# Dealing the tokens nine to a partition pair, loading the first batch in head halves, and a reordered first chain

## The chip, the cores and the metric

The kernel runs on one core of a Trainium2 chip. The metric is the device time of one execution in microseconds (us). The engines named here are PE (TensorE matmuls; PEld is its weight load), DVE (VectorE), ACT (ScalarE), POOL (GpSimd) and SP (SyncE, which only issues DMAs). Sixteen DMA engines serve all queues of the core. SBUF has 128 partitions; a "lower" tile lies in partitions 0 to 63, an "upper" one in 64 to 127.

## The reference

Eight batches, eight heads, 576 tokens, head size 64; then a mixer with rank 32 along the tokens and a hidden width of 2048.

```python
r = max(x, 0);  phi(x) = [r * cos(pi/2 * s/S), r * sin(pi/2 * s/S)]   # s: the token's position
kv  = einsum('bhsf,bhsd->bhfd', phi(k), v);  z = sum_s phi(k)
x   = einsum('bhsf,bhfd->bhsd', phi(q), kv) / (phi(q) . z + 1e-6)     # then [B, S, H*D]
u   = x + (x^T @ U @ V)^T                                            # U [576, 32], V [32, 576]
out = u + max(u @ w_ch1, 0) @ w_ch2                                  # [512 x 2048], [2048 x 512]
```

All inputs and the output are float32 in DRAM; matmuls run in bf16.

## The kernel before, in words

**Tokens.** 576 tokens are four and a half times 128. A batch is held as four chunks of 128 tokens and a tail of 64. Token 4p+c (p below 128, c below 4) is partition p of chunk c; tokens 512 to 575 are the tail, chunk 4, which lies in the lower partitions for even batches and the upper ones for odd batches, so that two batches share one tail tile (`tail`, L49). Every q, k or v of a batch is loaded by SP in two DMAs: `load_main` (L74, issued at L75; 128 partitions x 8 heads, 1 KB runs) and `load_tail` (L80, issued at L81; 64 partitions x 8 heads, 256 B runs). They land in float32 staging tiles `qst/kst/vst` and `qt/kt/vt` with one buffer each, so a batch's load waits until the one before has been read.

**The attention of a batch.** `q_prep` and `k_prep` (L246, L240) write relu(x) times cos and sin as bf16. `v_prep` and `v_block` cast v into `v_ext`, which has a column of ones for the denominator. `qtr_unit` (L273) transposes q on PE. `kv_unit` (L252) makes kv of four heads, `den_unit` and `recip` (L314, L310) the reciprocal denominators, `xh_unit` (L330) x for four heads of a chunk. `A_unit` (L374) multiplies by U, and `uTd_open`, `uTd_mm`, `uTd_evac` (L432 to L455) make the transposed u, which is what the mixer's first product reads.

**The mixer.** `g1_main` (L477, matmuls at L487) makes 16 tiles of the hidden layer of a batch from w_ch1 (`w1_bf`, four DMAs on POOL's queue at L91, cast to bf16 on the way), ACT applies the relu (L496). `g1_tail` (L500, matmuls at L507) does the shared tail of a pair. `g2_part` (L521, matmuls at L540) multiplies a chunk by w_ch2 (`w2_bf`, four DMAs at L97); DVE adds u (L550) into `o_sb` (four buffers), and one DMA per chunk writes 128 rows of 2 KB to `out` (L560), two DMAs of 64 rows for the shared tail (L556). The first three pairs write from POOL's queue; the last pair writes from SP's, and its last chunk in two parts, 384 columns from SP and 128 from ACT.

**The start.** The order is written by hand (`manual_schedule`), each engine works its own list from top to bottom. SP issues q, k, v of batch 0 (v in two halves of the heads), then V and U, then batch 1. POOL waits for k's tail (the copy into `mark`, L703), issues two of the four w_ch1 loads, casts V and U (`cast_uv`), issues the other two, then waits for k of batch 1 (L719) before the four w_ch2 loads. `chain_head`, `chain_mid` and `chain_end` (L645 to L685) are the first batch's attention, heads 0 to 3 ahead of heads 4 to 7, with `keep_warm` matmuls on zeros (L174) in the gaps of PE. Then `g1_main` of batch 0 starts. Later batches are laid beside the slots of the mixer by `attention_plan` and its table PLAN.

Of the kernel before, what the change touches and what calls it, by code (L numbers as in the profile page):

```python
# [17 lines left out]
def kernel(  # L18
# [29 lines left out]

    def tail(b):  # L49
        lo = TS * (b % 2)  # L50
        return slice(lo, lo + TS)
# [8 lines left out]
    kst, vst, qst, kt, vt, qt = {}, {}, {}, {}, {}, {}  # L60

    def alloc_k(b):
        kst[b] = pool.tile([P, H, 4, D], FP32, tag="kst", bufs=1, name="kst")
        kt[b] = pool.tile([P, H, D], FP32, tag="kt", bufs=1, name="kt")

    def alloc_v(b):
        vst[b] = pool.tile([P, H, 4, D], FP32, tag="vst", bufs=1, name="vst")
        vt[b] = pool.tile([P, H, D], FP32, tag="vt", bufs=1, name="vt")

    def alloc_q(b):  # L70
        qst[b] = pool.tile([P, H, 4, D], FP32, tag="qst", bufs=1, name="qst")
        qt[b] = pool.tile([P, H, D], FP32, tag="qt", bufs=1, name="qt")

    def load_main(dst, src, b, h0=0, h1=H, eng=None):  # L74
        (eng or nc.sync).dma_start(  # L75
            out=dst[:, h0:h1, :, :].rearrange("p h c d -> p h (c d)"),
            in_=src[b, h0:h1, 0:512, :].rearrange("h (p c) d -> p h (c d)", c=4),
        )

    def load_tail(dst, src, b, eng=None):  # L80
        (eng or nc.sync).dma_start(  # L81
            out=dst[tail(b), :, :],
            in_=src[b, :, 512:S, :].rearrange("h s d -> s h d"),
        )
# [16 lines left out]
    def cast(eng, o, i):  # L101
# [10 lines left out]

    alloc_k(0)
    alloc_q(0)
    alloc_v(0)
    iota = const.tile([P, 5], FP32)
    nc.gpsimd.iota(
        out=iota[:, 0:4], pattern=[[1, 4]], base=0, channel_multiplier=4,
        allow_small_or_imprecise_dtypes=True,
    )  # L120
    for lo in (0, TS):
        nc.gpsimd.iota(
            out=iota[lo : lo + TS, 4:5], pattern=[[1, 1]], base=512, channel_multiplier=1,
            allow_small_or_imprecise_dtypes=True,
        )
    load_main(qst[0], q, 0)
    load_tail(qt[0], q, 0)
    load_main(kst[0], k, 0)
    load_tail(kt[0], k, 0)
    load_tail(vt[0], v, 0)  # L130
    load_main(vst[0], v, 0, 0, 4)
    load_main(vst[0], v, 0, 4, 8)
    nc.sync.dma_start(out=stV, in_=moe_V)
    nc.sync.dma_start(
        out=stU[:, 0:4, :], in_=moe_U[0:512, :].rearrange("(p c) r -> p c r", c=4)
    )
    for lo in (0, TS):
        nc.sync.dma_start(out=stU[lo : lo + TS, 4, :], in_=moe_U[512:S, :])
# [7 lines left out]
    nc.scalar.activation(out=sinw, in_=iota, func=AF.Sin, bias=0.0, scale=scale_ang)  # L146
    nc.scalar.activation(out=cosw, in_=iota, func=AF.Sin, bias=halfpi, scale=-scale_ang)
# [14 lines left out]
    for i in range(2):  # L162
        V_.memset(v_ext[i][:, 4, :, :], 0.0)
        V_.memset(v_ext[i][:, 0:4, :, D:E], 1.0)
        V_.memset(v_ext[i][tail(i), 4, :, D:E], 1.0)
# [10 lines left out]
    V_.memset(U_bf, 0.0)  # L176
    mark = const.tile([TS, 1], FP32)
# [7 lines left out]
    def cast_uv():  # L185
        cast(G_, V_nat, stV)
        cast(G_, U_bf[:, 0:4, :], stU[:, 0:4, :])
        for i in range(2):
            cast(G_, U_bf[tail(i), 4 + i, :], stU[tail(i), 4, :])

    def spread_v(eng):
        v_ps = ps.tile([P, 2, 512], FP32, tag="X", bufs=1, name="v_ps")
        nc.tensor.matmul(
            out=v_ps[:, 0, :], lhsT=four, rhs=V_nat[:, 0:512], start=True, stop=True
        )
        nc.tensor.matmul(
            out=v_ps[:, 1, 0:TS], lhsT=four, rhs=V_nat[:, 512:S], start=True, stop=True
        )
        cast(eng, V_bf, v_ps[:, 0, :].rearrange("r (p c) -> r c p", c=4))
        cast(eng, V_tl, v_ps[:, 1, 0:TS])  # L200
# [5 lines left out]
    def v_prep(b, h0=0, h1=H, cs=range(5), engs=None):  # L206
        vx = v_ext[b % 2]
        for n, c in enumerate(cs):
            eng = engs[n] if engs else G_
            if eng is None:  # L210
                continue
            if c < 4:
                cast(eng, vx[:, c, h0:h1, 0:D], vst[b][:, h0:h1, c, :])
            else:
                cast(eng, vx[tail(b), 4, h0:h1, 0:D], vt[b][tail(b), h0:h1, :])

    def v_block(b, h0, h1, c0, c1, eng):
        cast(
            eng,
            v_ext[b % 2][:, c0:c1, h0:h1, 0:D].rearrange("p c h d -> p h c d"),  # L220
            vst[b][:, h0:h1, c0:c1, :],
        )
# [9 lines left out]
    def prep(dst, src, b, c, engs, h0, h1):  # L232
        rows = slice(0, P) if c < 4 else tail(b)
# [6 lines left out]
    def k_prep(b, c, engs, h0=0, h1=H):  # L240
        if b not in k_p:
            k_p[b] = pool.tile([P, 4, H, 2 * D], BF16, tag="k_p", bufs=1, name="k_p")
        src = kst[b][:, h0:h1, c, :] if c < 4 else kt[b][:, h0:h1, :]
        prep(k_p[b][:, c] if c < 4 else k_tl, src, b, c, engs, h0, h1)

    def q_prep(b, c, engs, h0=0, h1=H):  # L246
        if b not in q_p:
            q_p[b] = pool.tile([P, 4, H, 2 * D], BF16, tag="q_p", bufs=1, name="q_p")
        src = qst[b][:, h0:h1, c, :] if c < 4 else qt[b][:, h0:h1, :]
# [23 lines left out]
    def qtr_unit(b, c, h0=0, h1=H, eng=None, tag="T", bufs=1):  # L273
# [8 lines left out]
        if c < 4:  # L282
            cast(eng or V_, q_pT[b][:, c, h0:h1, :], t_ps[:, h0:h1, :])
        else:
            cast(eng or V_, q_tlT[:, h0:h1, tail(b)], t_ps[:, h0:h1, tail(b)])

    def qtr_dma(b, c0, c1):
# [6 lines left out]
        else:  # L294
            nc.sync.dma_start_transpose(
                out=q_tlT[:, :, tail(b)],
                in_=q_tl[tail(b), :, :].rearrange("p h f -> p (h f)"),
# [223 lines left out]
    def g2_part(pr, cc, part):  # L521
# [32 lines left out]
        if cc == 4:  # L554
            for i in range(2):
                eng.dma_start(  # L556
                    out=out[2 * pr + i, 512:S, :], in_=o_sb[i * TS : i * TS + TS, :]
                )
        else:
            eng.dma_start(  # L560
                out=out[b, 0:512, cols].rearrange("(p c) n -> p c n", c=4)[:, c, :],
# [4 lines left out]
    def loads(b, eng):  # L566
        def kk():
            alloc_k(b)
            load_tail(kt[b], k, b, eng)
            load_main(kst[b], k, b, eng=eng)  # L570

        def vv():
            alloc_v(b)
            load_tail(vt[b], v, b, eng)
            load_main(vst[b], v, b, eng=eng)

        def qq():
            alloc_q(b)
            load_tail(qt[b], q, b, eng)
            load_main(qst[b], q, b, eng=eng)  # L580

        return qq, kk, vv
# [21 lines left out]
    def attention_plan(b):  # L604
# [32 lines left out]
        for at, t in zip(lo, loads(b + 1, nc.sync) if lo else ()):  # L637
            plan.append((w + at, t))
# [6 lines left out]
    def chain_head(b, fill, xt, engs):  # L645
        v_prep(b, 0, 4, (4,), (engs[0],))
        v_block(b, 0, 4, 0, 3, V_)
        v_block(b, 0, 4, 3, 4, engs[0])
        kv_unit(b, 0, "T", 1)
        fill(0)  # L650
        rec0 = den_unit(b, 0, 4, "X", 1)
        v_prep(b, 4, 8, (4,), (A_,))
        v_block(b, 4, 8, 0, 4, A_)
        fill(1)
        for n, c in enumerate(ORD):
            xh_unit(b, c, 0, 4, rec0, *xt[n])
            if n == 1:
                fill(2)
            if n == 3:
                kv_unit(b, 1, "T", 1, A_)  # L660

    def chain_mid(b, fill, xt, dt):
        fill(3)
        m = 3
        rec1 = den_unit(b, 4, 8, *dt)
        for n, c in enumerate(ORD[:m]):
            xh_unit(b, c, 4, 8, rec1, *xt[n])
        u01 = ps.tile([P, 2, 512], FP32, tag="X", bufs=1, name="u01")
        uTd_open(b, 0, None, None, u01[:, 0, :].rearrange("p (c t) -> p c t", c=4))
        uTd_open(b, 1, None, None, u01[:, 1, :].rearrange("p (c t) -> p c t", c=4))  # L670
        a0 = A_unit(b, "T", 1, A_, 0, 256)
        fill(4)
        uTd_mm(b, 0)
        uTd_mm(b, 1)
        uTd_evac(b, 0, A_)
        uTd_evac(b, 1, A_)
        for n, c in enumerate(ORD[m:]):
            xh_unit(b, c, 4, 8, rec1, *xt[m + n])
        fill(5)
        return a0  # L680

    def chain_end(b, a0):
        A_unit(b, "T", 1, V_, 256, 512, a0)
        uTd_open(b, 2, "o", 2)
        uTd_open(b, 3, "o", 2)  # L685

    def warm0(n):
        m = (2, 1, 0, 1, 1, 2)[n]
        if m:
            keep_warm(m, *(O2 if n == 0 else G3))  # L690

    keep_warm(18, "X", 1)
    for c in TL:
        q_prep(0, c, (V_, V_ if c == 3 else A_))
    for n, c in enumerate(TL):
        qtr_unit(0, c, 0, H, (V_, A_, V_, A_, V_)[n], *(G3 if n < 3 else O2))
        if n in (1, 3):
            keep_warm(1, "X", 1)
    for c in TL:
        k_prep(0, c, (V_, V_ if c == 3 else A_))  # L700
    keep_warm(13, "o", 2)

    G_.tensor_copy(out=mark, in_=kt[0][0:TS, 0, 0:1])  # L703
    w1_load(0)
    w1_load(1)
    cast_uv()
    w1_load(2)
    w1_load(3)
    chain_head(0, warm0, (O2, O2, G3, G3, O2), (A_,))
    alloc_q(1)  # L710
    load_main(qst[1], q, 1)
    load_tail(qt[1], q, 1)
    alloc_k(1)
    load_tail(kt[1], k, 1)
    load_main(kst[1], k, 1)
    alloc_v(1)
    load_tail(vt[1], v, 1)
    load_main(vst[1], v, 1)
    G_.tensor_copy(out=mark, in_=kst[1][0:TS, 7, 3, 0:1])  # L719
    for n in range(4):  # L720
        w2_load(n)
    spread_v(A_)
    a0 = chain_mid(0, warm0, (O2, G3, O2, G3, O2), G3)
    chain_end(0, a0)
# [71 lines left out]
    for n, t in enumerate(loads(2, nc.sync)):  # L796
# [38 lines left out]
```

## Time and profile before

| | us |
|---|---|
| median of 3 runs (lowest, highest) | 313.55 (313.11, 314.17) |
| the profiled execution | 313.45 |
| its span, first to last instruction | 311.7 |
| PE busy | 303.7 (97% of the span) |
| DVE, ACT, POOL busy | 153.4, 137.5, 46.2 |
| mean share of the 16 DMA engines, queue of SP / of POOL | 57.2% / 15.1% |

Beside the profile's page the prediction uses these views: the chain of work that ended last, the waits by engine, the timeline, the table by stretches of time (busy time of each engine, granted clock, share of the sixteen DMA engines and GB/s moved), and the DMA view (packets and bytes of each queue in a stretch, and issues with the time to landing). A packet is one contiguous run on one DMA engine. The share can pass 1, because packets of different queues overlap on an engine.

### The profile page before, as it was taken

The page shows a single profiled execution, that of the slowest core. Times are in us where ns is not written, and L with a number is a line of the kernel's source. Part 1 is how long each engine was busy: PE and PEld are TensorE (multiplying, and loading weights), DVE is VectorE, ACT ScalarE, POOL GpSimd, SP SyncE. Part 2 cuts the span into 40 slices and gives each one's busy share as a digit, 9 for nine tenths or more (in the row PEclk, how much of TensorE's full clock was granted, in tenths as well). Part 3 has the DMA queues.
Part 4 walks back from the last instruction along what each step waited for, and adds up shares of the span by engine and source line. Part 5 has one row for each costly group of instructions (what it writes and reads, how often), then busy time and mean ns, then how long its engine had stood idle before and what let it go on. Part 6 is the DMA issues. An engine that isn't in the chain of part 4 may idle for free.

```text
span 311.7 us, 5648 instructions
## 1 busy us (share of the span) xinstructions
PE 303.7 (97%) x2314; PEld 157.6 (51%) x2314; DVE 153.4 (49%) x340; ACT 137.5 (44%) x229; POOL 46.2 (15%) x85
## 2 busy tenths in 40 slices
PE   7899989999999999999999999999999999999995
PEld 2566445445654444574455444484455444474443
DVE  5868835695878575046426584046426520002111
ACT  3846640265740366669400366669400366640000
POOL 2230300250031007003321400002320100000000
PEclk9999999999999999999999999999999999999999
DMA  7999999989996989992899589922871150001131
GB/s 215 281 244 228 254 183 257 325 200 247 273 178 131 265 200 208 234 306 60 187 226 306 209 103 211 304 76 53 180 157 69 67 86 0 0 2 67 67 103 67
DMA packets 88987, 53.21 MB, mean 171 GB/s; under 512 B 57122, under 2 KB 86178, under 8 KB 88962
## 3 DMA queue, kind: packets, MB, share of 16 engines
q1 hardware_dynamic: 82386, 41.52, 57.2%
q0 software_dynamic: 6432, 11.27, 15.1%
q8 instruction: 18, 0.29, 0.4%
q10 hardware_dynamic: 144, 0.07, 0.1%
q14 instruction: 7, 0.06, 0.0%
HBM read 36.86 MB, written 9.44 MB: 149 GB/s over the span
## 4 chain that ended last, share of the span: by engine, by line
PE 86%; issue 6%; DMA 4%; SPq 2%; POOL 1%; DVE 0%; POOLq 0%
PE o_ps L540 40%; PE g_ps L487 31%; PE gt_ps L507 5%; PE kv_ps L260 3%; PE x_ps L354 3%; DMA vst<-in_v_dram 2%; PE va_ps L399 2%; DMA w_bf<-in_moe_w_ch_dram 2%; SPq L81 1%; PE a_ps L379 1%; POOL w_bf L91 0%; PE va_ps L402 0%; SPq L75 0%; POOL U_bf L105 0%; PE d_ps L319 0%
## 5 line engine op out<-in xcount | busy, mean ns | idle before, releaser
L496 ACT ACTIVATE hid<-g_ps 128x512 bf16<-128x512 f32 x128 | 76.2, 597 | 105.5 <-PE g_ps L487 105.5
L540 PE MATMUL o_ps<-w_bf,hid 128*128 128x512 bf16 (+2 forms) x528 | 120.0, 372 | 1.0 <-DMA w_bf<-in_moe_w_ch_dram 1.0
L487 PE MATMUL g_ps<-uT,w_bf 128*128 128x512 bf16 x512 | 117.8, 379 | 0.1
L487 PEld LDWEIGHTS <-w_bf 128*128 128x128 bf16 x512 | 48.8, 98 | 58.0 <-issue 2.0
L540 PEld LDWEIGHTS <-hid 128*128 128x128 bf16 x528 | 48.2, 98 | 52.0 <-DMA w_bf<-in_moe_w_ch_dram 1.5
L550 DVE TENSOR_TENSOR o_sb<-u_bf,o_ps 128x512 f32<-128x512 bf16 (+2 forms) x33 | 22.0, 668 | 56.3 <-PE o_ps L540 56.2
L560 POOL DMA_DIRECT2D out_dram<-o_sb x24 | 13.2, 550 | 129.5 <-DVE o_sb L550 67.7
L406 DVE TENSOR_TENSOR u_bf<-x_bf,va_ps 128x512 bf16<-128x512 bf16 x32 | 21.9, 686 | 10.4 <-PE va_ps L399 10.4
L105 DVE CAST kv<-kv_ps 128x260 bf16<-128x260 f32 x15 | 6.4, 429 | 38.1 <-PE kv_ps L260 38.1
L364 DVE TENSOR_TENSOR x_bf<-x_ps,rec 128x512 bf16<-128x512 f32 x28 | 19.4, 691 | 1.0
L311 DVE TENSOR_SCALAR rec<-x_ps 128x8 f32<-128x8 f32 (+1 forms) x35 | 5.8, 165 | 22.8 <-PE x_ps L354 22.3
L507 PE MATMUL gt_ps<-uT_tl,w_bf 128*128 128x128 bf16 x256 | 15.9, 219 | 0.0
L507 PEld LDWEIGHTS <-w_bf 128*128 128x128 bf16 x256 | 14.7, 98 | 0.9
L540 PE MATMUL o_ps<-w_bf,hid_tl 128*128 128x512 bf16 x64 | 14.8, 379 | 0.0
L105 POOL CAST v_ext<-vst 128x512 bf16<-128x512 f32 x22 | 13.7, 653 | 3.6 <-DMA vst<-in_v_dram 3.4
L354 PEld LDWEIGHTS <-q_pT 128*128 128x128 bf16 x224 | 10.7, 98 | 6.4 <-DVE x_bf L364 0.4
L174 PE MATMUL w_ps<-zero 128*128 128x512 bf16 x40 | 11.6, 422 | 1.8 <-DVE halfpi L142 1.2
L226 ACT ACTIVATE k_p<-kst,sinw 128x512 bf16<-128x512 f32 x19 | 13.3, 708 | 0.0
L260 PEld LDWEIGHTS <-k_p 128*128 128x128 bf16 x256 | 11.2, 97 | 3.9 <-ACT v_ext L103 0.7
L228 DVE TENSOR_SCALAR q_p<-qst,cosw 128x512 bf16<-128x512 f32 x24 | 12.0, 513 | 2.1 <-DMA qst<-in_q_dram 2.0
L514 ACT ACTIVATE hid_tl<-gt_ps 128x512 bf16<-128x512 f32 x16 | 9.6, 597 | 6.6 <-PE gt_ps L507 6.6
L260 PE MATMUL kv_ps<-v_ext,k_p 128*128 128x65 bf16 x256 | 11.8, 193 | 0.4 <-DVE v_ext L105 0.4
(104 smaller groups left out, 234.2 us busy)
## 6 DMA issues: line engine op xcount, KB each, us to landing
qst<-in_q_dram SPq DMA_DIRECT2D x8, 1024.0 KB, 7.6
kst<-in_k_dram SPq DMA_DIRECT2D x8, 1024.0 KB, 10.3
vst<-in_v_dram SPq DMA_DIRECT2D x7, 1024.0 KB, 10.0
out_dram<-o_sb POOLq DMA_DIRECT2D x24, 256.0 KB, 3.7
w_bf<-in_moe_w_ch_dram POOLq DMA_DIRECT2D x8, 512.0 KB, 11.6
out_dram<-o_sb SPq DMA_DIRECT2D x7, 256.0 KB, 2.3
qt<-in_q_dram SPq DMA_DIRECT2D x8, 128.0 KB, 4.2
kt<-in_k_dram SPq DMA_DIRECT2D x8, 128.0 KB, 7.8
```

The source lines that it names most:

```text
L105: eng.tensor_copy(out=o, in_=i)
L226: nc.scalar.activation(out=o, in_=i, func=AF.Relu, bias=0.0, scale=w)
L260: nc.tensor.matmul(out=acc[:, i, :], lhsT=k_p[b][:, c, h, :] if c < 4 else k_tl[:, h, :], rhs=vx[:, c, h, :], start=(c == 0), stop=(c == 4),)
L354: nc.tensor.matmul(out=acc[:, g, i * E : i * E + E], lhsT=qT_of(b, c, h), rhs=kv_sb[b][:, h, :], start=True, stop=True,)
L364: nc.vector.tensor_tensor(out=x_of(b, c, rows).rearrange("p (g i d) -> p g i d", g=2, d=D), in0=view[:, :, :, 0:D], in1=rec[rows].unsqueez ...
L406: nc.vector.tensor_tensor(out=u_bf[b][:, c, :] if c < 4 else u_tl[b // 2], in0=x_of(b, c), in1=va, op=ALU.add,)
L487: nc.tensor.matmul(out=g_ps.rearrange("p (c t) -> p c t", c=4), lhsT=w1_bf[:, d, j * P : j * P + P], rhs=uT[b][:, :, d, :], start=(d == 0) ...
L496: nc.scalar.activation(out=hid[b][:, j, :], in_=g_ps, func=AF.Relu, bias=0.0, scale=1.0)
L507: nc.tensor.matmul(out=g_ps[:, jj, :], lhsT=w1_bf[:, d, j * P : j * P + P], rhs=uT_tl[pr][:, d, :], start=(d == 0), stop=(d == 3),)
L540: nc.tensor.matmul(out=o[:, cols], lhsT=lhs[:, j, c * P : c * P + P], rhs=w2_bf[:, j, cols], start=(j == 0), stop=(j == NJ - 1),)
L550: nc.vector.tensor_tensor(out=o_sb[:, cols], in0=u[:, cols], in1=o[:, cols], op=ALU.add)
L560: eng.dma_start(out=out[b, 0:512, cols].rearrange("(p c) n -> p c n", c=4)[:, c, :], in_=o_sb[:, cols],)
```

## The change

1. **Tokens.** Token 9m+k (m below 64, k below 9) is now lower partition m, chunk k, for k of 0 to 4, and upper partition 64+m, chunk k-5, for k of 5 to 8. Chunk 4, the tail, is thus always in the lower partitions of the staging tile. A batch's q, k or v is one tile of five chunks, loaded as a lower DMA (64 partitions, 1280 B runs) and an upper one (64 partitions, 1024 B runs). The tables of angles, `cast_uv`, `spread_v`, U's layout and the writes to `out` follow. A main chunk of `out` is now written by one DMA whose destination is a pattern of 2 x 64 rows x 512, the rows of a half 9 x 2 KB apart.
2. **Start of the loads.** q of batch 0 is loaded in two halves of the heads, the lower parts from SP's queue and the upper ones from ACT's. U and V go to POOL's queue ahead of everything else there. v of batches 0 and 1 is loaded in halves of the heads, four DMAs each.
3. **Gates.** POOL casts U and V first, then waits for the lower half of v's heads 0 to 3 of batch 0, issues all four w_ch1 loads, and waits for the same part of batch 1's v before the four w_ch2 loads.
4. **Chain.** q is prepared and transposed by halves of the heads. `first_chain` casts both halves of v and makes both kv units first, then both denominators, then x of heads 0 to 3, x of heads 4 to 7, A and the transposed u. Its `keep_warm` matmuls are gone; those ahead of it are 9, 2, 2 and 13.

```diff
-    def load_main(dst, src, b, h0=0, h1=H, eng=None):
-        (eng or nc.sync).dma_start(
-            out=dst[:, h0:h1, :, :].rearrange("p h c d -> p h (c d)"),
-            in_=src[b, h0:h1, 0:512, :].rearrange("h (p c) d -> p h (c d)", c=4),
-        )
-    def load_tail(dst, src, b, eng=None):
...
+    def load(dst, src, b, h0=0, h1=H, engs=(nc.sync, nc.sync)):
+        nines = src[b].rearrange("h (m k) d -> m h (k d)", k=9)[:, h0:h1]
+        for eng, rows, k0, n in zip(engs, (LO, HI), (0, 5), (5, 4)):
+            eng.dma_start(
+                out=dst[rows, h0:h1, 0:n, :].rearrange("m h c d -> m h (c d)"),
+                in_=nines[:, :, k0 * D : k0 * D + n * D],
+            )
...
-    load_main(qst[0], q, 0)
-    load_tail(qt[0], q, 0)
-    load_main(kst[0], k, 0)
-    load_tail(kt[0], k, 0)
-    load_tail(vt[0], v, 0)
-    load_main(vst[0], v, 0, 0, 4)
-    load_main(vst[0], v, 0, 4, 8)
-    nc.sync.dma_start(out=stV, in_=moe_V)
...
+    for h0 in (0, 4):
+        load(qst, q, 0, h0, h0 + 4, (nc.sync, nc.scalar))
+    load(kst, k, 0)
+    for h0 in (0, 4):
+        load(vst, v, 0, h0, h0 + 4)
+    def load_uv():
+        nc.gpsimd.dma_start(out=stV, in_=moe_V)
...
             eng.dma_start(
-                out=out[b, 0:512, cols].rearrange("(p c) n -> p c n", c=4)[:, c, :],
+                out=out[b].rearrange("(m k) n -> k m n", k=9)[c : c + 6 : 5, :, cols],
                 in_=o_sb[:, cols],
             )
...
+    def first_chain(b):
+        v_block(b, 0, 4, 0, 3, V_)
+        v_block(b, 0, 4, 3, 4, A_)
+        v_prep(b, 0, 4, (4,), (A_,))
+        v_block(b, 4, 8, 0, 3, V_)
+        v_block(b, 4, 8, 3, 4, A_)
+        v_prep(b, 4, 8, (4,), (A_,))
+        kv_unit(b, 0, *T1)
+        kv_unit(b, 1, *O2, A_)
...
+        den_mm(b, 0, 4, d[0])
+        den_mm(b, 4, 8, d[1])
+        x0 = [xh_mm(b, c, 0, *t) for c, t in zip(ORD, (G3, G3, G3, O2, O2))]
+        recip(rec[0], d[0])
...
-    G_.tensor_copy(out=mark, in_=kt[0][0:TS, 0, 0:1])
-    w1_load(0)
-    w1_load(1)
     cast_uv()
-    w1_load(2)
-    w1_load(3)
-    chain_head(0, warm0, (O2, O2, G3, G3, O2), (A_,))
+    G_.tensor_copy(out=mark, in_=vst[0:TS, 3, 4, 0:1])
+    for n in range(4):
+        w1_load(n)
+    first_chain(0)
...
-    G_.tensor_copy(out=mark, in_=kst[1][0:TS, 7, 3, 0:1])
+    load(vst, v, 1, 0, 4)
+    load(vst, v, 1, 4, 8)
+    G_.tensor_copy(out=mark, in_=vst[0:TS, 3, 4, 0:1])
     for n in range(4):
         w2_load(n)
```

## Prediction

> **What bounds the kernel.** The executed time is 313.45 us, its span 311.7, so 1.75 lie around the span; the runs' median is 313.55, and what I work out on the execution holds for it within 0.1. I read the page first:
>
> ```profile
> PE 303.7 (97%) x2314; PEld 157.6 (51%) x2314; DVE 153.4 (49%) x340; ACT 137.5 (44%) x229; POOL 46.2 (15%) x85
> ...
> PE 86%; issue 6%; DMA 4%; SPq 2%; POOL 1%; DVE 0%; POOLq 0%
> ...
> out_dram<-o_sb SPq DMA_DIRECT2D x7, 256.0 KB, 2.3
> ```
>
> PE carries the end, but 40 of its matmuls (11.6 us, L174) are on zeros and stand in the start. So I cut the span into stretches, the last column being GB/s and the one before it the share of the sixteen DMA engines:
>
> ```profile
> 0.00:22.90 22.90, 19.47 (x235) 11.35 (x236) 15.63 (x45) 13.18 (x23) 6.59 (x22) 1.00 1.03 248
> 22.90:41.75 18.85, 17.75 (x116) 9.04 (x113) 14.83 (x30) 12.91 (x23) 3.26 (x5) 1.00 1.10 227
> 41.75:309.00 267.25, 266.52 (x1968) 137.17 (x1968) 122.99 (x266) 111.40 (x185) 36.37 (x58) 1.00 0.68 161
> 309.00:311.70 2.70, 0.00 (x0) 0.00 (x0) 0.00 (x0) 0.00 (x0) 0.00 (x0) 0.94 0.24 79
> ```
>
> From 41.75 to 309 PE is full: nothing that the change does there can gain, it can only break in. The two early stretches have the DMA engines full, and the tail after PE's last matmul is 2.7 us. The chain in order of time, and PE's waits, say what ends the early part:
>
> ```profile
> 6.45 7.51 DMA vst<-in_v_dram
> ...
> 36.16 5.54 DMA w_bf<-in_moe_w_ch_dram
> 41.70 0.05 issue
> 41.75 1.04 PE o_ps L540 x4
> ```
> ```profile
> PE o_ps L540 <- DMA w_bf<-in_moe_w_ch_dram: 1.0, 1, 1.0
> ```
>
> v of heads 0 to 3 lands at 13.96 and starts the chain; `g1_main` begins at 22.98; PE then runs dry at 40.70 and waits 1.04 us for the first w_ch2 load. So the start ends at the later of two: the chain plus 17.7 us of PE work, or the 41.70 at which that load lands. A chain that is quicker by itself gains nothing, a chain up to 1.04 slower costs nothing.
>
> **Prices of a DMA packet.** Three more stretches: one 128-row output, the two 64-row outputs of the tail, and q and k alone.
>
> ```profile
> 303.00:303.50 0.50, 0.50 (x4) 0.21 (x3) 0.00 (x0) 0.00 (x0) 0.00 (x0) 1.00 1.00 381
> 296.60:297.40 0.80, 0.80 (x6) 0.39 (x4) 0.00 (x0) 0.00 (x0) 0.00 (x0) 1.00 0.86 192
> 3.20:4.80 1.60, 1.60 (x6) 0.60 (x5) 1.49 (x5) 0.00 (x0) 0.00 (x0) 1.00 1.06 370
> 2.00:16.00 14.00, 11.99 (x99) 6.41 (x98) 9.99 (x25) 8.54 (x17) 2.79 (x7) 1.00 1.09 284
> ```
>
> The DMA view counts 93 packets of 2 KB in the first and 75 in the second: 16 x 0.50 x 1.00 / 93 = 86 ns each with 128 partitions, 16 x 0.80 x 0.86 / 75 = 147 ns with 64. At a full share the 64-partition rate is 192 / 0.86 = 222 GB/s against 381.
>
> The Trainium skill ("SBUF — State Buffer", Door 1: the DMA port swizzle) has a cause: partitions 0 to 63 reach eight of sixteen DMA ports; with half of 435 GB/s as ceiling it agrees with the 222 and speaks against loads by halves.
>
> **Part by part.**
>
> *Writes to out.* The program of the change has the destination as 2 x 64 rows where it was 128 rows. Nothing in the trace shows how a transfer with so small an outermost count is dealt to the engines; all that fill sixteen of them have 64 or 128 outermost. Two ends. (a) Dealt by rows: 128 packets on 16 engines as now, cost 0. (b) Dealt by the outermost count: two engines of 64 packets, 64 x 86 = 5.5 us for 256 KB, where PE makes a chunk every 3.45 (issues at 298.65, 302.10, 305.56). I take (b), the end nearer to the rows of 147 and 86 ns: they look as if a transfer's outermost entries were dealt out in order, 128 or 64 partitions over sixteen engines, so that with 64 all sixteen sit on one half of SBUF; nothing looks as if inner entries were dealt. For the first three pairs the price is hidden: a chunk has four buffers, 13.8 us, against 5.5 + 1.6, and the queue drains in the next pair's `g1_main`. The last pair has no later work to hide under. From its first issue at 281.38 the two engines hold 7 chunks x 5.5 = 38.5, the tail 2 x 4 packets x 147 ns = 1.2, 384 columns 64 x 65 ns = 4.1, 128 columns 64 x 22 ns = 1.4: 45.2 in all, and 1.6 for the way there and back (2.3 less 128 / 16 x 86 ns). 281.4 + 45.2 + 1.6 = 328.2, where the last write now lands at 308.65 + 1.8 = 310.4. Cost **17.8**.
>
> The Trainium skill ("DMA: Bandwidth & Descriptors", Rules for kernel authors) says that a small outermost dimension confines a DMA to at most so many engines. By it the count is two and the sum as in (b); no run here shows it yet.
>
> *Loads of batch 0.* Before, 3.7 MB went at 284 GB/s, with the last half of v landed at 15.71. After: q's halves come from two queues at once, so both halves of SBUF are written, 1.18 MB at 370 = 3.2; U and V 0.15 MB = 0.4, ahead of nothing the chain needs early; k and v on SP alone, lower then upper, 1.18 MB at 222 = 5.3 each. From 2.0: q at 5.2, with U and V 5.6, k 10.9, v's heads 0 to 3 13.6, heads 4 to 7 16.2, each landing some 0.7 later: 14.3 and **16.9** (13.96 and 15.71 before). q's earlier half buys q_prep 1 to 2 us, but k_prep then waits for k at 11.6, where it began at 10.98. If the halves do not bind, everything is in at 2 + 3.7 / 0.370 = 12, 3.7 us sooner. If w_ch1's packets start before v ends, v's last 16 packets or so per engine each wait one of about 96 ns: up to 1.8 more, 18.7. (In before the first of them came only at 17.4, 5.2 after the issue.)
>
> *Chain.* From v's second half, by rows of the chain before: v_block 0.56, kv 0.78, two denominators 1.30, add 0.18, norm 0.42, reciprocal 0.28, four norms 1.40, A 0.45 + 0.38, transposed u 0.25 + 0.55, ten hops 0.4: 7.0, against 22.98 - 15.71 = 7.3. So `g1_main` starts at 23.9 to 25.7, 0.9 to 2.7 late, less the 1.04 of slack: 0 to 1.7. With the fill matmuls gone PE stands idle up to 2 to 3 us before kv; the clock was 1.00 throughout before, so no row prices that: between 0 and, at double time for the chain's matmuls, 3 us; 0 taken, the row nearest.
>
> *Gates.* w_ch1 is issued at 13.1 instead of 12.23 and 17.41, w_ch2 when the lower half of heads 0 to 3 has landed instead of all of k. Against w_ch1's packets each packet takes a turn: 1536 per tensor before, 1024 after. From 22 to 24 us the DMA view has 311 packets on POOL's queue (93.0% of 16 x 2 us, 96 ns each) and 309 on SP's (29.5%, 31 ns each): turn about, so a tail packet of 256 B holds a whole turn. Leaving out batch 1's three tails, 3 x 32 packets per engine, is at most 3 us. Against it stand the later gate (the lower part of half of v more, 0.33 MB, 1.5 us at 222 GB/s) and the dearer lower and upper packets, up to 1.7-fold where no w_ch1 packet lies between. w_ch2 lands at 39 to 43; I take 41 to 42.5, -0.7 to +0.8.
>
> *Sum for the start:* the later of the two, 0 to 2, below that if the halves do not bind; I take **+1.0**.
>
> *Later batches.* Loads of batch 3 are the tight ones: POOL casts v at 86.83 straight on landing, and PE takes it at 90.28. A slower 1.18 MB per tensor, 5.3 against some 4.5, is 2 us late over three; ACT and POOL have about 2 there. 0 taken, up to 1.
>
> Sum: 313.45 + 17.8 + 1.0 = **332.2**.
>
> **Rivals.**
> - *Outputs dealt by rows, halves bind* (0.22): only the start's +1.0 and batch 3's: 314.5, 313 to 317. For it: POOL's writes today move two rows in one packet (0.26 MB in 80 packets from 237 to 241 us, 16 of them completions), so that queue at least looks at rows.
> - *Outputs by rows, halves do not bind* (0.13), the one that ends faster: packets of 1 KB and more only, v in 3 us sooner, `g1_main` at 20, w_ch2 at 39. It decides as soon as v's second half lands before 15. Bounded by w_ch2's DMA time: 311.3.
> - *POOL's writes too on the same two engines* (0.05): the four at 57 to 62 us last 22 us, to 80, and the loads of batch 3, issued from 70, are late by some 4 at 90.28: 336.5.
>
> **Chances.** Forecast (b) with the start at 0 to 2: 0.60, own range 328 to 336. To leave out no more than 2 in 10 the range must reach down into the second case: 313 to 337. Faster by over 0.3% (0.94 us, about what a measurement tells): 0.13. Within: 0.08, of the second case. Slower: 0.79.
>
> **What would show it.** Right: after 281 us a queue of SP with few of sixteen engines busy (share near 0.12, some 48 GB/s), DMA running on for about 18 us after PE's last matmul, landings of the output growing by 2 us per chunk. In 6 to 16 us rates near 220 GB/s; v's second half at 16.9; `g1_main` at 24 to 26. Wrong: outputs landing in 2.3 us, or 350 GB/s while k loads alone.

## The result, and the profile after

The changed kernel takes 384.62 us (median; 380.67 to 386.6) against 313.55 (312.45 to 314.17) for the kernel before, run beside it: a ratio of 1.221, 95% interval 1.213 to 1.230. Ratios, here and below, are of the means and leave out executions that fell into a slower state (386.6 here), so they differ a little from those of the medians. The profiled execution has a span of 383.4. The forecast was 332.2, its range ended at 337.

The page of the changed kernel, the same places as before: PE's busy share, the clock row, the queue of POOL, the chain by engine, the output's landing (the last number, us).

```profile
PE 318.7 (83%) x2274; PEld 163.7 (43%) x2300; DVE 152.1 (40%) x346; ACT 136.4 (36%) x234; POOL 62.8 (16%) x91
...
PEclk9969999997898599999988998999978899999965
...
q0 software_dynamic: 17312, 11.52, 15.2%
...
PE 55%; DMA 29%; SPq 7%; DVE 2%; ACT 1%; issue 1%; POOL 0%; DVEq 0%
...
out_dram<-o_sb POOLq DMA_DIRECT2D x24, 256.0 KB, 14.2
```

PE is idle in the middle of the kernel as well, and slow: the clock row has dips where it was full. POOL's writes need 14.2 us to land (3.7 before), although they hold no more bytes. Its queue now has 17312 packets (6432 before): packet by packet, each main chunk is 64 packets of 4 KB and 448 of 8 bytes. A row has 2 KB and the rows of a half lie 18 KB apart, so a packet on POOL's queue need not be one contiguous run. In the kernel before:

```profile
q0 software_dynamic: 6432, 11.27, 15.1%
...
out_dram<-o_sb POOLq DMA_DIRECT2D x24, 256.0 KB, 3.7
```

The table by stretches, cut at the first `g1_main`, the first `g2_part`, batch 2's `g1_main` and PE's last matmul (columns as in the prediction):

```profile
0.00:29.46 29.46, 21.19 (x220) 13.44 (x222) 17.01 (x51) 13.38 (x28) 9.48 (x28) 0.88 1.02 221
29.46:46.82 17.36, 17.36 (x111) 9.09 (x112) 13.47 (x29) 11.45 (x21) 3.15 (x5) 1.00 1.17 229
46.82:126.42 79.60, 63.38 (x543) 33.95 (x550) 42.70 (x99) 22.66 (x38) 19.34 (x18) 0.93 1.14 171
126.42:364.34 237.92, 216.81 (x1403) 107.19 (x1418) 78.60 (x166) 88.96 (x148) 30.87 (x40) 0.94 0.84 119
364.34:383.40 19.06, 0.00 (x0) 0.00 (x0) 0.29 (x1) 0.00 (x0) 0.00 (x0) 0.59 0.12 46
```

The span is 71.7 longer, in three parts. **Start:** the first `g2_part` at 46.82 instead of 41.75, +5.1. **Middle:** 317.5 from there to PE's last matmul (364.34), where it was 266.5 (41.75 to 308.30): +51. **End:** 19.06 after it, where it was 3.4: +15.7. Of the middle's 51, PE's idle time is about 37 (317.5 less 63.4 and 216.8 busy); the other 14 or so are matmuls that take longer, at a clock of 0.93 and 0.94 instead of 1.00. PE's waits name what it idles for (total, times, longest, us); two of DVE's stand below them:

```profile
PE x_ps L369 <- DMA q_pT<-q_p: 17.6, 4, 4.8
PE g_ps L502 <- DMA uT<-u_bf: 10.2, 2, 7.8
PE x_ps L369 <- DVE x_tl L379: 6.1, 1, 6.1
...
PE g_ps L502 <- DMA w_bf<-in_moe_w_ch_dram: 1.1, 1, 1.1
```
```profile
DVE q_tl L230 <- DMA qst<-in_q_dram: 7.4, 1, 7.4
...
DVE o_sb L565 <- DMA out_dram<-o_sb: 2.6, 1, 2.6
```

The first two are transposes that SP issues as DMAs. Nothing in them was changed, and in the kernel before PE never waits for them. The third goes back to them: DVE works in order and waited 7.4 us for q of batch 3, whose load SP issued only at 85.4, after standing at three transposes from 70.5 on. The DMA view shows what holds the transposes, in four stretches of the changed kernel (queue: packets, MB, share of sixteen engines). From 107 to 109 us there are transposes alone:

```profile
q1 hardware_dynamic: 2286, 0.58, 127.7%
```

From 116 to 122 POOL's writes move beside them:

```profile
q1 hardware_dynamic: 578, 0.15, 101.4%
q0 software_dynamic: 142, 0.20, 12.2%
```

From 118.5 to 121.5, a part of that stretch, 26 of the 31 packets on POOL's queue are those of 4 KB:

```profile
DMA packets 275, 0.17 MB, mean 56 GB/s; under 512 B 249, under 2 KB 249, under 8 KB 275
...
q1 hardware_dynamic: 244, 0.06, 120.0%
q0 software_dynamic: 31, 0.11, 9.6%
```

From 122 to 123.5 none are, and only small ones move:

```profile
DMA packets 1149, 0.27 MB, mean 182 GB/s; under 512 B 1149, under 2 KB 1149, under 8 KB 1149
...
q1 hardware_dynamic: 1095, 0.27, 122.6%
q0 software_dynamic: 54, 0.00, 2.8%
```

A transpose moves in packets of 256 B. The share passes 1 here with one queue alone, so packets of one queue overlap too, and I go by packets per us: 1143 alone, 96 and 81 beside the packets of 4 KB, 730 beside small ones. The pace falls with the packets of 4 KB and not with the many small ones. From 124 to 126 us POOL's queue moves 46 packets of 4 KB and nothing else:

```profile
q0 software_dynamic: 46, 0.19, 22.9%
```

One takes 0.229 x 16 x 2.0 us / 46 = 159 ns, and a packet of a transpose alone 1.277 x 16 x 2.0 / 2286 = 18 ns. An estimate from these two: if each packet of a transpose waits for one of 4 KB on the engines that a write holds, and the transpose goes no faster than these engines, sixteen engines move 16 / 0.177 us = 90 packets per us, near the 96 and 81. The trace has no engine numbers, so which packet waits for which is read from the pace and not seen.

### The profile page after: what moved, and what is told of

It reads as the page before. It is cut to its first block, busy times and chain, and to the rows that moved or that the text cites. A ratio compares the mean times of both kernels' runs of the same rounds, so it can differ in the third digit from the quotient of the medians.

```text
span 383.4 us, 5622 instructions
## 1 busy us (share of the span) xinstructions
PE 318.7 (83%) x2274; PEld 163.7 (43%) x2300; DVE 152.1 (40%) x346; ACT 136.4 (36%) x234; POOL 62.8 (16%) x91
## 3 DMA queue, kind: packets, MB, share of 16 engines
q0 software_dynamic: 17312, 11.52, 15.2%
## 4 chain that ended last, share of the span: by engine, by line
PE 55%; DMA 29%; SPq 7%; DVE 2%; ACT 1%; issue 1%; POOL 0%; DVEq 0%
PE g_ps L502 23%; PE o_ps L555 22%; DMA vst<-in_v_dram 9%; DMA q_pT<-q_p 5%; DMA uT<-u_bf 5%; DMA uT_tl<-u_tl 4%; SPq L68 3%; DMA w_bf<-in_moe_w_ch_dram 3%; SPq L305 3%; DMA out_dram<-o_sb 3%; PE gt_ps L522 3%; PE kv_ps L262 2%; PE x_ps L369 2%; PE va_ps L414 1%; ACT k_p L228 1%
## 5 line engine op out<-in xcount | busy, mean ns | idle before, releaser
L502 PE MATMUL g_ps<-uT,w_bf 128*128 128x512 bf16 x512 | 122.0, 389 | 11.4 <-DMA uT<-u_bf 10.2
L555 PE MATMUL o_ps<-w_bf,hid 128*128 128x512 bf16 (+2 forms) x509 | 124.1, 386 | 1.3 <-issue 0.4
L502 PEld LDWEIGHTS <-w_bf 128*128 128x128 bf16 x512 | 49.6, 100 | 72.3 <-DMA uT<-u_bf 11.2
L555 PEld LDWEIGHTS <-hid 128*128 128x128 bf16 x528 | 49.9, 101 | 54.6 <-issue 7.8
L576 POOL DMA_DIRECT2D out_dram<-o_sb x24 | 19.5, 813 | 139.2 <-DVE o_sb L565 114.2
L92 POOL CAST v_ext<-vst 128x512 bf16<-128x512 f32 (+1 forms) x28 | 27.5, 1012 | 67.5 <-DMA vst<-in_v_dram 67.5
L369 PE MATMUL x_ps<-kv,q_pT 128*128 128x65 bf16 x224 | 13.5, 208 | 23.7 <-DMA q_pT<-q_p 17.6
L421 DVE TENSOR_TENSOR u_bf<-x_bf,va_ps 128x512 bf16<-128x512 bf16 x32 | 21.9, 686 | 11.7 <-PE va_ps L414 10.8
L369 PEld LDWEIGHTS <-q_pT 128*128 128x128 bf16 x224 | 11.9, 108 | 32.7 <-DMA q_pT<-q_p 19.5
L555 PE MATMUL o_ps<-w_bf,hid_tl 128*128 128x512 bf16 x61 | 16.3, 413 | 0.2
L522 PEld LDWEIGHTS <-w_bf 128*128 128x128 bf16 x256 | 14.7, 98 | 1.6 <-DMA uT_tl<-u_tl 0.9
L230 DVE TENSOR_SCALAR q_p<-qst,cosw 128x512 bf16<-128x512 f32 (+1 forms) x28 | 11.7, 438 | 3.9 <-DMA qst<-in_q_dram 3.9
## 6 DMA issues: line engine op xcount, KB each, us to landing
out_dram<-o_sb POOLq DMA_DIRECT2D x24, 256.0 KB, 14.2
```

The source lines that it names most:

```text
L92: eng.tensor_copy(out=o, in_=i)
L369: nc.tensor.matmul(out=acc[:, g, i * E : i * E + E], lhsT=qT_of(b, c, h), rhs=kv_sb[b][:, h, :], start=True, stop=True,)
L421: nc.vector.tensor_tensor(out=u_bf[b][:, c, :] if c < 4 else u_tl[b // 2], in0=x_of(b, c), in1=va, op=ALU.add,)
L502: nc.tensor.matmul(out=g_ps.rearrange("p (c t) -> p c t", c=4), lhsT=w1_bf[:, d, j * P : j * P + P], rhs=uT[b][:, :, d, :], start=(d == 0) ...
L522: nc.tensor.matmul(out=g_ps[:, jj, :], lhsT=w1_bf[:, d, j * P : j * P + P], rhs=uT_tl[pr][:, d, :], start=(d == 0), stop=(d == 3),)
L555: nc.tensor.matmul(out=o[:, cols], lhsT=lhs[:, j, c * P : c * P + P], rhs=w2_bf[:, j, cols], start=(j == 0), stop=(j == NJ - 1),)
```

## The experiments

Names of the theories: **W**, the 2 x 64 writes are held by two engines each and keep SP's transposes from moving; **L**, the loads by halves come late throughout; **C**, PE cooled in the start and stays so. H, K, G and O concern the start alone: what sets its end is the loads by halves (H), the cooled PE (K), the later gates (G) or the new order of the chain (O). Differences are against `before` run beside each kernel.

**split_all.** The one write of a main chunk becomes two of 64 rows, all else as changed.

```diff
-                out=out[b].rearrange("(m k) n -> k m n", k=9)[c : c + 6 : 5, :, cols],
-                in_=o_sb[:, cols],
+            nines = out[b].rearrange("(m k) n -> k m n", k=9)
+            for i, rows in enumerate((LO, HI)):
+                eng.dma_start(out=nines[c + 5 * i, :, cols], in_=o_sb[rows, cols])
```

> Each main chunk of the output goes in two DMAs of 64 rows (outermost count 64) instead of one of 2 x 64 rows; all else as in the changed kernel. Theory W (the 2 x 64 writes sit on two DMA engines and hold up SP's transposes there): the middle's +51 and the end's +15.7 go, the start's +5.1 stays: 313.5 + 5.1 = 318.6, from 317 to 320. Rival L (the loads by partition halves come late for every batch): only the end's 15.7 goes, 384.6 - 15.7 = 369. Rival C (PE cooled in the start, where the fill matmuls are gone, and its clock stays low): also 365 to 370.

Measured 320.53 (320.01 to 320.73), ratio 1.021 (1.018 to 1.023). 64 of the 71 us are gone, with the same rows, runs and bytes. In its table by stretches the middle is full again (third row), and the write of 128 KB lands in 4.4:

```profile
0.00:29.10 29.10, 19.25 (x221) 11.70 (x223) 16.91 (x51) 13.43 (x28) 9.48 (x28) 0.88 1.03 214
29.10:46.45 17.35, 17.35 (x110) 9.09 (x111) 13.58 (x29) 11.45 (x21) 3.15 (x5) 1.00 1.18 238
46.45:314.80 268.35, 265.61 (x1945) 137.33 (x1967) 121.13 (x265) 111.52 (x186) 51.73 (x82) 1.00 0.81 159
314.80:318.90 4.10, 0.00 (x0) 0.00 (x0) 0.29 (x1) 0.00 (x0) 0.00 (x0) 1.00 0.29 64
```

And its page, for the write:

```profile
out_dram<-o_sb POOLq DMA_DIRECT2D x54, 128.0 KB, 4.4
```

The start keeps its 0.88 and its lateness (46.45), yet the middle runs at 1.00: C and L fall as causes of the middle. Against the span of before, 4.7 stay in the start, 1.8 in the middle and 0.7 in the end.

**split_pool** and **split_last.** The same edit for the first three pairs alone (`if pr < NPAIR - 1`), and for the last pair alone.

> Only the writes of the first three pairs, on POOL's queue, are split in two DMAs of 64 rows. Theory W: the middle's +51 goes, the start and the end stay: 313.5 + 5.1 + 15.7 = 334.3, from 332 to 337. Rivals L and C: nothing goes, 384.

> Only the writes of the last pair, on the queues of SP and ACT, are split in two DMAs of 64 rows. Theory W: only the end's 15.7 goes: 384.6 - 15.7 = 369, from 366 to 372, with the same gaps of PE from 85 to 300 us. Rivals L and C: 369 as well; so this run tells whether the end is worth what the sum gave it, and whether end and middle add up.

Measured 335.57 (335.18 to 335.81) and 367.29 (366.71 to 371.43). From split_all to split_pool it is 15.0: the end by itself. From the changed kernel to split_last it is 17.3, the end again. From split_all to split_last it is 46.8: the middle by itself. 15.0 and 46.8 add up to 61.8 of the 64.1 between split_all and the changed kernel, whose own runs lie 5.9 apart.

**before_2x64.** The kernel before, and only the pattern of the write changed; rows of the upper half are stored at the next chunk's places, so that the two halves can't be one even pattern.

```diff
+            r = 257 if c < 3 else 253
...
-                out=out[b, 0:512, cols].rearrange("(p c) n -> p c n", c=4)[:, c, :],
+                out=out[b, c : c + 2 * r].rearrange("(i r) n -> i r n", r=r)[:, 0:253:4, cols],
```

> The kernel before (its loads, tokens, chain), and only the writes of main chunks have a destination of 2 x 64 rows: the upper 64 rows of a chunk go to the next chunk's places, so those rows of the output stand in another order; bytes, DMAs, queues and runs of 2 KB as before. Theory W (such a write is held by two engines, and alone holds up SP's transposes): middle and end of the changed kernel's loss, 313.5 + 51 + 15.7 = 380, from 372 to 388. Rival W2 (the middle's loss needs the slower loads by halves beside the writes): the end and less than half of the middle, 329 to 350.

Measured 380.72 (375.01 to 381.58), ratio 1.201 (1.193 to 1.210). One line of the change carries all but some 5 us of its price (66.3 of 71.1). The last two stretches of its table, middle and end:

```profile
43.04:354.29 311.25, 279.16 (x1969) 139.46 (x1968) 121.39 (x265) 112.59 (x187) 48.15 (x58) 0.95 0.78 136
354.29:378.30 24.01, 0.00 (x1) 0.00 (x0) 0.29 (x1) 0.00 (x0) 0.00 (x0) 0.58 0.11 41
```

Against the span of before the middle is 44.7 longer and the end 20.6 (51 and 15.7 in the changed kernel): the sum came as expected, the two parts only roughly.

PE's waits in it, the two longest sums:

```profile
PE g_ps L487 <- DMA uT<-u_bf: 15.2, 3, 6.9
PE x_ps L354 <- DMA q_pT<-q_p: 5.2, 2, 3.8
```

And the write, on its page:

```profile
out_dram<-o_sb POOLq DMA_DIRECT2D x24, 256.0 KB, 11.2
```

The same two transposes are late, with 128-partition loads: W2, which needs the halves, falls.

**before_load_2x64.** The kernel before, q of batch 4 in eight DMAs whose source is 2 x 64 runs (tokens of the upper partitions shifted by one).

```diff
+        if dst is qst.get(4):
+            for h in range(h0, h1):
+                (eng or nc.sync).dma_start(
+                    out=dst[:, h, :, :].rearrange("p c d -> p (c d)"),
+                    in_=src[b, h, 0:514, :].rearrange("(i r) d -> i r d", i=2)[
+                        :, 0:256, :
+                    ].rearrange("i (p c) d -> i p (c d)", c=4),
+                )
+            return
```

> The kernel before, with q of batch 4 loaded head by head, in eight DMAs of 128 KB whose source is 2 x 64 runs of 1 KB (the upper partitions get their tokens shifted by one). If it is the outermost count of the pattern that deals the packets, whatever the direction, each of them holds two engines for 64 x 50 ns = 3.2 us, 25.6 for the eight, and the last lands 26 us or more after the issue. If only writes to the output are dealt so: all eight in about 1.05 MB at 350 GB/s = 3 us, landing 8 us after the issue as now. The time itself: 313.5 to 316, since q of batch 4 has slack.

Measured 331.23 (one execution). The packets behave as W says: the last of the eight lands at 129.6, 27.5 us after the first was issued. The DMA view from 112 to 122 us, SP's queue alone on the engines:

```profile
DMA packets 480, 0.48 MB, mean 48 GB/s; under 512 B 8, under 2 KB 480, under 8 KB 480
...
q1 hardware_dynamic: 480, 0.48, 13.6%
```

And the longest of PE's waits in it:

```profile
PE g_ps L496 <- DMA uT<-u_bf: 15.3, 1, 15.3
```

13.6% of sixteen engines is 2.2 of them, at 48 GB/s. It is the pattern's outermost count, on a read as on a write. The expected time was missed: q of batch 4 has slack, but SP issues in order, stood 2.6 to 3.3 us at each of the later ones of these DMAs, and batch 3's transposes, which PE needs, stood behind them (the first at 129.2; their u was ready at 114.5).

**before_halves.** The kernel before, every main load of q, k and v in two DMAs of 64 partitions.

```diff
+        for lo in (0, TS):
+            (eng or nc.sync).dma_start(
+                out=dst[lo : lo + TS, h0:h1, :, :].rearrange("p h c d -> p h (c d)"),
+                in_=src[b, h0:h1, 4 * lo : 4 * lo + 256, :].rearrange(
+                    "h (p c) d -> p h (c d)", c=4
+                ),
+            )
```

> The kernel before, with each main load of q, k and v in two DMAs, partitions 0 to 63 and 64 to 127, one after the other on the same queue; tokens, writes and chain as before. Theory W: the halves cost something in the start alone, where three tensors of 1.05 MB at 222 instead of some 284 GB/s put v's last half about 2.5 us later, less 1.04 of slack: 313.5 to 316, nothing in the later batches. Rival L: the later batches are late too, as in the changed kernel: 350 or more. Rival C: no word on this one, 313.5.

Measured 329.93 (328.04 to 333.6), ratio 1.049 (1.045 to 1.053): far more than expected. Some 10 us of it stand in the start (first `g2_part` at 51.83), 5.0 of them in one wait of PE that I had not looked for (ACT itself waits for q's tail; the chain that ended last has 5% of the span on that load):

```profile
PE t_ps L280 <- ACT q_tl L229: 5.0, 1, 5.0
```

Batch 1's tail of q lies behind all of batch 0 on SP's queue. The rest of the traced growth, 4.5 of 14.6, comes behind the start, where nothing was expected; 2.2 of it PE waits for v_ext of batch 3. The halves cost 10 in the start here and 4.7 in split_all, which has no tails of 256 B to load. That the tails make the difference is argued and not shown: gates, chain and q's second queue differ as well.

Three rates, in stretches with SP's loads: before from 7.5 to 9 us (1 KB packets, 128 partitions), split_all from 11.5 to 14.5 (1 and 1.25 KB, one half of the partitions at a time) and from 4 to 9, where q's halves were to come from two queues side by side.

```profile
7.50:9.00 1.50, 1.40 (x20) 1.14 (x21) 1.50 (x5) 1.50 (x4) 0.00 (x0) 1.00 1.09 359
```

And split_all:

```profile
11.50:14.50 3.00, 2.95 (x20) 1.41 (x17) 0.87 (x2) 1.27 (x2) 0.24 (x2) 1.00 1.12 228
4.00:9.00 5.00, 3.06 (x21) 1.16 (x19) 2.02 (x8) 1.58 (x5) 2.17 (x8) 1.00 1.11 227
```

359 GB/s against 228. And two queues gave q no more, 227: from 5 to 6 ACT's queue moved 212 packets and SP's 3, from 6.5 to 9 SP's 398 and ACT's none, so for most of the time one half of SBUF was written. Where two queues do move side by side, the rate is higher. split_two_queues, described below, has k and v on two queues; from 9 to 16 it reaches 311 GB/s (split_both 307), where split_all has 225:

```profile
9.00:16.00 7.00, 5.04 (x38) 2.83 (x40) 4.63 (x13) 5.05 (x9) 0.65 (x3) 1.00 1.12 225
```

And split_two_queues:

```profile
9.00:16.00 7.00, 5.76 (x41) 2.95 (x40) 5.55 (x15) 5.97 (x10) 1.41 (x6) 1.00 1.09 311
```

**The start: split_two_queues, split_fills, split_gates, split_both.** All from split_all: k and v with their upper halves on ACT's queue; matmuls on zeros in PE's holes; earlier gates; all three (fills 20 and 5).

```diff
-    load(kst, k, 0)
+    load(kst, k, 0, engs=(nc.sync, nc.scalar))
-        load(vst, v, 0, h0, h0 + 4)
+        load(vst, v, 0, h0, h0 + 4, (nc.sync, nc.scalar))
```
```diff
-    keep_warm(13, "X", 1)
+    keep_warm(27, "X", 1)
...
         kv_unit(b, 0, *T1)
+        keep_warm(7, "X", 1)
```
```diff
-    cast_uv()
-    G_.tensor_copy(out=mark, in_=vst[0:TS, 3, 4, 0:1])
+    G_.tensor_copy(out=mark, in_=kst[0:TS, 0, 4, 0:1])
+    w1_load(0)
+    w1_load(1)
+    cast_uv()
...
-    G_.tensor_copy(out=mark, in_=vst[0:TS, 3, 4, 0:1])
+    G_.tensor_copy(out=mark3[HI], in_=kst[HI, 7, 3, 0:1])
```

> As split_all (320.5), and k and v of batch 0 have their upper halves on ACT's queue, so that both halves of SBUF are written at once. Theory H (in the start the halves loaded in series set the end): v's second half lands at 16 to 17 instead of 19.7, all that follows comes 3 us sooner: 317.5, from 316.5 to 318.5. Rival K (the cooled PE in the chain is what is late): at most 1 us gained, 319.5 to 320.5. Rival G (the later gates of w_ch1 and w_ch2): the gates are v's landings and move with them, so 317.5 as well.

> As split_all, and PE has matmuls on zeros in the two holes of the start: 27 instead of 13 ahead of kv of heads 0 to 3, and 7 between that and kv of heads 4 to 7. Rival K: kv, denominators and x take 0.59 us per 16 or 0.28 per 4 matmuls again instead of up to 1.04 and 0.41, the chain is 1.5 to 2 us shorter, and the time is 318.5 to 319. Theories H and G: the granted clock and the durations come back all the same, but w_ch1 lands at 29.05 as before and PE waits there some 2 us instead of 0.8: 320 to 320.5.

> As split_all, and POOL waits for the lower half of k of batch 0 (landing at 12.2) instead of that of v's heads 0 to 3 (16.0) before w_ch1, and for the upper half of k of batch 1 (35.7) instead of v (38.0) before w_ch2; two w_ch1 loads go ahead of the casts of V and U. Rival G: the wait of 0.83 for w_ch1 goes, w_ch2 comes 2 us sooner, nothing else is late: 319 to 319.7. Theory H: v's packets meet w_ch1's, v lands up to 1.8 later and so the chain: 320.5 to 322. Theory K: 320.5, no change.

> All three together: two queues for k and v of batch 0, fills (20 and 5) and the earlier gates. If the three limits of the start lie beside each other (each alone is covered by the next), this gains more than the sum of the single ones: the chain of 7 to 9 us from v's second half at 16 to 17 puts g1_main at 24 to 25.5 as in the kernel before or 2 us behind it, 315 to 316.5. If H alone is the limit: as split_two_queues, 317.5.

| kernel | median (lowest, highest) us | ratio to before, 95% | v's last half, w_ch1's first, g1_main at |
|---|---|---|---|
| split_all | 320.53 (320.01, 320.73) | 1.018 to 1.023 | 19.7, 29.05, 29.1 |
| split_two_queues | 322.07 (317.9, 323.66) | 1.014 to 1.024 | 17.0, 27.4, 27.4 |
| split_fills | 321.21 (321.06, 324.05) | 1.021 to 1.027 | 19.95, 29.6, 29.7 |
| split_gates | 320.45 (320.44, 320.6) | 1.018 to 1.023 | 20.0, 25.4, 28.85 |
| split_both | 317.78 (317.24, 319.89) | 1.009 to 1.016 | 17.7, 26.0, 26.7 |

No single one gains anything that shows; the three together gain some 2.5 (3.8 above the kernel before run beside it, where split_all is 6.3). Each limit lies behind another: in split_two_queues v is 2.7 sooner and PE then waits 2.1 for w_ch1; in split_gates w_ch1 is 3.7 sooner and the chain is not ready. split_two_queues stays unclear: its runs spread over 5.8 us, and why is open; its times in the table are from an execution of 323.4.

The clock is real but lay under that cover. The stretch from 14.7 to 25.2 us, first of split_all:

```profile
14.70:25.20 10.50, 5.55 (x118) 4.96 (x118) 6.77 (x19) 4.58 (x10) 3.53 (x5) 0.73 1.13 229
```

split_fills:

```profile
14.70:25.20 10.50, 9.83 (x154) 6.28 (x153) 7.09 (x20) 5.25 (x12) 3.54 (x5) 1.00 1.13 225
```

0.73 granted without the fills, 1.00 with them; from the first cast of v to A it is 8.3 and 7.2 us. In split_all PE idles 3.2 us, makes kv of heads 0 to 3 at full pace (0.28 us per four matmuls), idles 1.8, and makes kv of heads 4 to 7 at 0.38 to 0.41.

The Trainium skill ("TensorE: Matmul & The Clock Gate", Why this matters for your kernels) wants no idle gap of PE over some 3 us between bursts. The trace agrees in part: the first hole was 3.2 us, but the pace fell only behind the second, shorter one, with 0.7 us of work between them.

**both_old_chain.** split_both with `chain_head`, `chain_mid`, `chain_end` and their fills in place of `first_chain`.

```diff
-    first_chain(0)
+    chain_head(0, warm0, (O2, O2, G3, G3, O2), (A_,))
...
+    spread_v(A_)
+    a0 = chain_mid(0, warm0, (O2, G3, O2, G3, O2), G3)
+    chain_end(0, a0)
```

> As split_both (317.8; there g1_main starts 9.0 us after v's second half), with the chain of the kernel before (both denominators apart, the second kv behind x of heads 0 to 3; 7.3 us from v's second half there). Rival O (the new order itself makes the chain longer): g1_main 1.7 sooner, 316. Theory H (the order costs nothing, the loads by halves and their 222 GB/s do): 317.8, within 0.5.

Measured 318.81 (318.01 to 319.79), ratio 1.012 to 1.017, beside split_both's 1.009 to 1.016. O falls: the new order costs nothing that shows. With the old one `g1_main` starts at 27.7, 1.0 later than in split_both, where O would have it 1.7 sooner; the time is 1.0 above split_both, more than the 0.5 that H allowed.

**before_w2_early.** The kernel before with an earlier gate for w_ch2.

```diff
-    G_.tensor_copy(out=mark, in_=kst[1][0:TS, 7, 3, 0:1])
+    G_.tensor_copy(out=mark3[TS:P], in_=kt[1][TS:P, 0, 0:1])
```

> The kernel before, and POOL waits for the tail of k of batch 1 (landing at 29.0) instead of all of k (36.0) before the four w_ch2 loads. If the first w_ch2 load is all that ends the start, PE's wait of 1.04 us goes and nothing else comes late: 312.5. If w_ch2's packets, seven us sooner, hold up batch 1's k and v, which PE needs right behind: 313.5 to 315.

Measured 323.56 (322.99 to 324.3), ratio 1.030 (1.027 to 1.032): the second case, and dearer than I had put it. The wait for w_ch2 goes, v of batch 1 lands at 48.8 instead of 39.2, and PE stands:

```profile
PE kv_ps L261 <- DVE v_ext L105: 8.3, 2, 7.0
```

None of these versions beats the kernel before.

## Why the prediction was wrong, point by point

- **Writes dealt by the outermost count (b): right.** From 369 to 381 us of the changed kernel only SP's and ACT's writes run, and the DMA view has two engines' worth of work, (0.115 + 0.018) x 16 = 2.1:

```profile
DMA packets 420, 0.60 MB, mean 50 GB/s; under 512 B 6, under 2 KB 236, under 8 KB 420
...
q1 hardware_dynamic: 290, 0.53, 11.5%
q10 hardware_dynamic: 130, 0.07, 1.8%
```

  The rule of the Trainium skill that the prediction weighed ("DMA: Bandwidth & Descriptors", Rules for kernel authors) holds here, with two engines for an outermost count of two.
- **The end, +17.8: right in mechanism and nearly in size.** From the first issue (337.42) to the end of the span are 46.0 us, where the sum had 45.2 + 1.6. The measured growth is 15.7 in the trace, 15.0 by split_pool against split_all; the rest of the difference is that the sum took off the last landing of before (310.4) and not the end of its span.
- **The step that failed: "For the first three pairs the price is hidden: a chunk has four buffers, 13.8 us, against 5.5 + 1.6, and the queue drains in the next pair's `g1_main`."** It asked only whether POOL and its buffers could wait. They can: DVE waits for a buffer once, 2.6 us. It did not ask who else needs those engines while the queue drains. SP's transposes of q and u do, in just these stretches (PE waits 27.8 us for them), and then the loads behind them on SP (6.1 us by way of DVE). Price 46.8 by split_last against split_all, where 0 was taken.
- **The rival "POOL's writes too on the same two engines" (336.5): the right place, one tenth of the size.** It counted the loads of batch 3 as late by some 4, on the time that the writes hold two engines. It left out that a transpose is spread over all sixteen engines (its share in the view is 101%) and goes at 81 to 96 packets per us instead of 1143, that this comes in every one of the three pairs, and that a PE that waits so loses clock: 0.93 and 0.94 in the two stretches of the middle, the 14 us of slower matmuls, against 1.00 in split_all. Whether POOL's writes sit on SP's two engines is not shown; from 124 to 126 us its 4 KB packets (22.9% of sixteen) fill 3.7 engines, from 118.5 to 121.5 (9.6%) 1.5, so that one or two writes at a time seem to have two engines each.
- **Start, +1.0 (bounds 0 to 2): too small, +5.1 (4.7 in split_all).** Two of its terms. q's halves "from two queues at once" at 370 GB/s came at 227 (split_all) and 256 (the changed kernel, 4 to 9 us), since the two queues took turns for most of the time, q's second half at 9.4 instead of 5.2 to 5.9, and v's last half at 19.8 instead of 16.9. The chain, put at 7.0 from there, took 9.7: 1.1 is the clock by split_fills against split_all (0.73 there, taken at nothing, bound 3), 1.1 the wait for w_ch1, whose gate is later; the other 0.5 is open.
- **The 222 GB/s of loads by halves: right** (228 in split_all, 359 with 128 partitions). "Halves do not bind" falls. That the 222 "agrees" with half of 435 as a ceiling holds only roughly: the half is 217.5, and 222 and 228 lie above it.
- **Later batches, 0 up to 1:** 1.8 in split_all, of which PE waits 1.4 for v of batch 3 at 95 us.
- **The signs for "wrong" named landings of 2.3 us and fast loads,** the hopeful side only. A wait of PE in the middle was not among the signs.

## What to carry to other kernels

Look at the outermost count of a DMA's pattern on both sides before its bytes: 2 x 64 rows in one DMA cost 66 us in the kernel before (380.7 against 314.4), and with the same rows in two DMAs of 64 the changed one is 1.8 us longer in the middle and 0.7 at the end. When a transfer gets slow but "has time", ask what else passes through the engines and the queue that it holds, above all transfers that are spread over all engines and that PE waits for. In a start with several limits at once, an edit to one of them shows nothing by itself; a table of landings tells which one is next.

## What the runs showed of the hardware that I had not expected

- A 2 x 64 write on POOL's queue is cut otherwise than on SP's: 64 packets of 4 KB (159 ns) and 448 of 8 bytes, against 128 packets of 2 KB at 84 ns.
- A transpose that is spread over all engines slows down on the whole (1143 to 81 packets per us), while the other queue fills 9.6% of the engines' time.
- SP stands at its issue while earlier DMAs are still moving: up to 10.8 us at one transpose in the changed kernel (from 190.5 us on), 2.6 to 3.3 us per 128 KB read in before_load_2x64. The kernel before shows it too: 8.9 us at v's tail of batch 1 (from 16.2 us on).
- Two queues that load one half each don't keep both halves of SBUF busy by themselves: q came at 227 GB/s, as with one queue. Where both had packets to move, k and v came at 311 and 307 (split_two_queues and split_both, 9 to 16 us).
